# Pooled keys and values of two batches summed by TensorE, and a scale moved into the keys

## The chip, the cores and the metric

The kernel runs on one core of a Trainium2 chip. The metric is the device time in microseconds (us) of one execution.

## The reference

Attention over pooled keys and values, and then two feed-forward blocks. All inputs are fp32 or wider in DRAM (the weights come as 64-bit floats); q and k are drawn eight times larger than v.

```python
q, k, v: (8 batches, 8 heads, 576 rows, 64)
k_p = k.reshape(B, H, 72, 8, 64).mean(axis=3)      # v_p likewise
scores = (q @ k_p^T) / sqrt(64)
attn = softmax(scores, axis=-1)
x = (attn @ v_p) as (4608 tokens, 512)
h = ((x @ w1) * (x @ w2)) @ w3 @ w_out1            # 512 -> 1024 -> 512
y = relu(h @ w_in)**2 @ w_out                      # 512 -> 2048 -> 512
```

## The kernel before, in words

There are 4608 tokens in nine blocks of 512 (`TB`); a batch has 576 tokens, in five query tiles of 128 rows or 64 (`QT`), the first two and the last three of which form a half. Work goes in three parts that overlap.

*The fold.* `fold` multiplies w3 with the first w_out beforehand. `conv_w3` and `conv_wo` read 64-bit weights (`load64`, into `raw` tiles), ScalarE and four VectorE instructions of `to32` make two fp32 parts of each (tiles `v` for w3, summed into `wo`), and TensorE transposes the parts of w3 by fp32 matmuls with the identity (L542) and multiplies with wo (L565). The first group takes three blocks of w3 rows at once, the later ones one each. `load_split` converts the first half of w1 and w2 in the fold's later part.

*Attention.* `build_tasks` writes out a list of small steps; `tick`, which is called after every few matmuls, takes the next 0.6 to 0.7 of them, so that attention is spread among the matmuls of the other parts. For each batch `load_k` and `load_v` bring 128 pooled rows at a time, 8 x 64 numbers each (2 KB in a row), into tiles of a pool of three that the weights use as well, and VectorE sums each with one reduce (L248). GpSimd doubles the sums of k, `pe_kt` transposes them on TensorE, and copies put them in block-diagonal form into `kbd`. The sums of v are split by VectorE into a high and a low part (`vhl`), and 16 short DMAs per batch put them into `vl` (the first 128 pooled rows of each pair of heads) and `vr` (the 16 rows left). Then for each query tile `pe_s` makes scores of four heads at a time, their maximum (L351), its product with -scale (L352) and the exponentials (L354); `pe_t` transposes them and `pe_av` multiplies with `vl` and `vr`. For batches below `EARLY` = 2, q is loaded in natural layout and transposed on TensorE (L313); for the others VectorE transposes it.

*The token blocks.* `stage_ab` and `stage_w` run the first feed-forward block, from TensorE's view 24 matmuls of 512 columns for w1 and w2 and 12 for the folded weight, then `stage_h`, `stage_o` and `pair_group` the second. The second half of w1 and w2 (`fh1`) is converted while the first token block runs, stored to DRAM (L185) and read back in the order of use through a ring of eight tiles (`fetch`, `un`, L195). That ring stands empty until the fourth step of the first block.

Instructions are put in order per engine by a scheduler that follows the code's order unless a step would wait. Nearly all DMAs go through SP's queue, which issues in order; an instruction that waits for a buffer holds up those behind it.

Of the kernel before, what the change touches and what calls it, by code (L numbers as in the profile page):

```python
# [29 lines left out]
def attn_moe_moe2_kernel(  # L30
# [77 lines left out]
    def f32(ap):  # L108
        return ap.bitcast(F32)
# [98 lines left out]
    vl = at_p.tile([P, 2, NP, 2, D], F32R, tag="vl", name="vl")  # L208
    vr = at_p.tile([RR, NP, 2, D], F32R, tag="vr", name="vr")
    kbd = at_p.tile([P, NP, 2, SP], F32, tag="kbd", name="kbd")  # L210
    att = [at_p.tile([P, H * SP], F32, tag=f"att{i}", name=f"att{i}") for i in range(2)]

    def setup_consts():
        make_identity(nc, ident)
        nc.gpsimd.memset(f32(vl), 0.0)
        nc.gpsimd.memset(f32(vr), 0.0)
        nc.gpsimd.memset(kbd, 0.0)
        nc.gpsimd.memset(vp, 0.0)


    xt = {}
# [8 lines left out]
    atts = {}  # L230
    sums = {}
    rems = {}
    def kv_rows(j):
        return P if j < NJ - 1 else JL

    def load_kv(src, b, dst, j):
# [10 lines left out]
                    r[c * RM:(c + 1) * RM], flat[c * 2 * SP + P:(c + 1) * 2 * SP])  # L247
        nc.vector.reduce_sum(dst[:n], r[:n].rearrange("p r d -> p d r"), axis=AX.X)  # L248

    def load_k(b):  # L250

        for j in range(NJ):
            load_kv(k, b, kp[:, j, 0, :], j)
        nc.gpsimd.tensor_copy(kp[:, :NJ - 1, 1, :], kp[:, :NJ - 1, 0, :])
        nc.gpsimd.tensor_copy(kp[:JL, NJ - 1, 1, :], kp[:JL, NJ - 1, 0, :])

    def load_v(b):


        for j in range(NJ):  # L260
            load_kv(v, b, vp[:, j, :], j)
        nc.vector.tensor_copy(vhl[:, 0].bitcast(F32R), vp)
        nc.vector.tensor_sub(vp.bitcast(F32R), vp, vhl[:, 0])
        for par, (r0, r1) in enumerate(((0, SP), (SP, P))):
            for i in range(2):
                nc.sync.dma_start(f32(vl)[r0:r1, i, :, par, :], vhl[r0:r1, i, :NP, :])
        for c in range(NP):
            for i in range(3):
                r0 = i * RB + c % 2 * RM
                nc.sync.dma_start(  # L270
                    f32(vr)[r0:r0 + RM, c, 1, :], vhl[c * RM:(c + 1) * RM, i // 2, NP, :])
        done.add(("v", b))

    def pe_kt(b, part):


        ps = ps_at.tile([P, TB], F32, tag="at", name="ps_kt")
        n = (NJ - 1) * P
        c0 = (H - 1) * SP
        if part == 0:  # L280
            for j in range(NJ - 1):
                nc.tensor.transpose(
                    ps[:, j * P:(j + 1) * P], kp[:, j].rearrange("p a d -> p (a d)"), ident)
            nc.scalar.copy(kbd[:D, :, 0, :], runs(ps[:D], 0, 2 * SP, NP, SP))
            nc.scalar.copy(kbd[D:, :NP - 1, 1, :], runs(ps[D:], SP, 2 * SP, NP - 1, SP))
            nc.scalar.copy(kbd[D:, NP - 1, 1, :n - c0], ps[D:, c0:n])
            return
        nc.tensor.transpose(
            ps[:, :JL], kp[:JL, NJ - 1].rearrange("p a d -> p (a d)"), ident[:JL, :JL])
        nc.vector.tensor_copy(kbd[D:, NP - 1, 1, n - c0:], ps[D:, :JL])  # L290
        if b + 1 < B:
            load_k(b + 1)

    def runs(ap, off, step, n, w):

        a = ap[:, off:off + (n - 1) * step + w]
        return bass.AP(tensor=a.tensor, offset=a.offset, ap=[a.ap[0], [step, n], [1, w]])
# [29 lines left out]
    def pe_s(g, half):  # L327
# [17 lines left out]
        if half == 0:  # L345
            sums[g] = at_p.tile([P, H], F32, tag="sm", name="sm", bufs=2)
        sm = sums[g]

        scale = 1.0 / (POOL * D ** 0.5)

        nc.vector.reduce_max(mx[:n], sv, axis=AX.X)  # L351
        nc.vector.tensor_scalar(mx[:n], mx[:n], -scale, None, op0=ALU.mult)  # L352
        for h in range(NP):
            nc.scalar.activation(  # L354
                av[:, h0 + h], sv[:, h], ACTF.Exp, bias=mx[:n, h:h + 1], scale=scale,
                accum_out=sm[:n, h0 + h:h0 + h + 1])
        if half == 0:
            return
# [67 lines left out]
    def build_tasks():  # L426
# [24 lines left out]
        for g in range(NG):  # L451
# [9 lines left out]
                sc(g + 1)  # L461
            if i == HALF[hf][0]:
                put_pend(len(pend))
            for part in range(2):
                put(lambda g=g, part=part: pe_t(g, part))
                put_pend()
# [47 lines left out]
    def fold():  # L514
# [33 lines left out]
        for fs in groups:  # L548
# [3 lines left out]
            for h in range(nm // nh):  # L552
# [8 lines left out]
                for m in range(h * nh, (h + 1) * nh):  # L561
                    if first:
                        conv_wo(m)
                    for f in fs:
                        nc.tensor.matmul(  # L565
                            acc_w[f], w3t[f][:, m, :], wo_t[m // 2][:, m % 2, :],
                            start=m == 0, stop=m == nm - 1)
                        tick()
                    n += 1
                    if n == 4:  # L570
                        start_attention()
                    if n == 6:
# [17 lines left out]
    def stage_ab(i, u):  # L590
# [1 line left out]
        cs = slice(c * P, (c + 1) * P)  # L592
        pss = []
        if (i, u) == (0, TB // P - 1):
            until(lambda: not fh1)
            for _ in range(RING):
                fetch()
        for nm_ in ("w1", "w2"):
# [439 lines left out]
```

## Time and profile before

| | |
|---|---|
| median of three runs | 1645.61 us (1643.55 to 1647.1) |
| profiled execution, its own time | 1649.5 us |
| span of the profiled execution | 1647.6 us |
| TensorE busy (matmuls / weight loads) | 1583.2 us (96%) / 1261.8 us (77%) |
| VectorE busy | 940.3 us (57%) |
| ScalarE busy | 549.3 us (33%) |
| GpSimd busy | 164.8 us (10%) |
| mean granted TensorE clock | 0.987 of full speed |
| SP's DMA queue | 213888 packets, 212.28 MB |

The time is that of the whole execution, the span runs from its first to its last instruction. Shares are over the whole span; the stretches differ, so what an edit is worth is read from the stretch that it lies in. A granted clock of 1.0 is 2.4 GHz and 0.5 is 1.2 GHz.

### The profile page before, as it was taken

The numbers are of one execution on the slowest core, as the hardware profiler recorded it, in microseconds if no ns is written. First come the engines' busy times: TensorE is split into PE (matmuls) and PEld (weight loads), VectorE is DVE, ScalarE is ACT, GpSimd is POOL, SyncE is SP. The second block draws the span as 40 slices with busy tenths as digits, with TensorE's granted clock in tenths as the row PEclk, the third lists the DMA queues.
The fourth block names the chain that finished last, engine by engine and source line by source line (L and its number), as shares of the span: only waits on it lengthen the run. The fifth ranks groups of instructions, "written<-read, shape, count | busy, mean of one in ns | idle before, by whom it ended". The sixth has DMA issues, their size and how long they took to land.

```text
span 1647.6 us, 20821 instructions
## 1 busy us (share of the span) xinstructions
PE 1583.2 (96%) x7136; PEld 1261.8 (77%) x7136; DVE 940.3 (57%) x1658; ACT 549.3 (33%) x1485; POOL 164.8 (10%) x202
## 2 busy tenths in 40 slices
PE   7889789989999999999899999999999999999998
PEld 5456578777778778788688888888888888888887
DVE  8798756665765555636742535464546455645542
ACT  4454425444444343434322321132113211331121
POOL 1132301211111111112410000000000000000000
PEclk9999899999999999999999999999999999999999
DMA  8454575736475825542634444342444244414410
GB/s 261 142 156 131 158 212 139 205 105 188 126 201 156 261 72 163 142 123 65 222 102 118 134 131 126 117 129 82 128 119 128 83 127 123 123 43 130 127 64 26
DMA packets 218601, 222.00 MB, mean 135 GB/s; under 512 B 93056, under 2 KB 134016, under 8 KB 218496
## 3 DMA queue, kind: packets, MB, share of 16 engines
q1 hardware_dynamic: 213888, 212.28, 44.4%
q10 hardware_dynamic: 4608, 8.39, 1.4%
q8 instruction: 57, 0.93, 0.2%
q14 instruction: 48, 0.39, 0.1%
HBM read 179.31 MB, written 38.80 MB: 132 GB/s over the span
## 4 chain that ended last, share of the span: by engine, by line
PE 50%; DMA 0%; ACT 0%; issue 0%; DVE 0%; DVEq 0%
PE o L162 24%; PE ps_a L861 5%; PE ps_c L861 5%; PE ps_d L861 5%; PE ps_h L162 3%; PE ps_w L162 3%; PE ps_b L861 3%; PE acc L162 2%; DMA out_dram<-st 0%; DVE st L778 0%; ACT raw L136 0%; ACT st L780 0%; ACT asb L615 0%; DVEq L778 0%; ACT wt L113 0%
## 5 line engine op out<-in xcount | busy, mean ns | idle before, releaser
L162 PE MATMUL o<-wt,gt 128*128 128x512 f32 x1728 | 413.6, 394 | 0.0
L162 PEld LDWEIGHTS o<-wt,gt 128*128 128x128 f32 x1728 | 323.8, 188 | 77.1 <-ACT gt L113 1.2
L162 PE MATMUL ps_w<-x,un 128*128 128x512 f32 x864 | 222.2, 405 | 16.2 <-DMA un<-u_w 10.2
L162 PE MATMUL ps_w<-x,wt 128*128 128x512 f32 x864 | 228.6, 405 | 6.5 <-ACT x L415 2.3
L162 PE MATMUL acc<-gt,Wt 128*128 128x512 f32 x864 | 219.5, 397 | 1.0 <-ACT st L646 1.0
L162 PEld LDWEIGHTS ps_w<-x,un 128*128 128x128 f32 x864 | 163.2, 193 | 52.5 <-DMA un<-u_w 11.7
L162 PEld LDWEIGHTS ps_w<-x,wt 128*128 128x128 f32 x864 | 157.8, 190 | 42.0 <-DVE x L418 5.0
L162 PEld LDWEIGHTS acc<-gt,Wt 128*128 128x128 f32 x864 | 159.6, 189 | 35.1 <-ACT st L646 1.8
L354 ACT ACTIVATE att<-ps_s,mx 128x72 f32<-128x72 f32 (+1 forms) x320 | 98.2, 319 | 88.3 <-DVE mx L352 86.0
L861 PE MATMUL ps_a<-x2o,un 128*128 128x512 f32 x384 | 98.4, 391 | 0.0
L861 PE MATMUL ps_c<-x2o,un 128*128 128x512 f32 x384 | 97.5, 389 | 0.0
L861 PE MATMUL ps_d<-x2o,un 128*128 128x512 f32 x384 | 97.4, 389 | 0.0
L886 ACT ACTIVATE r<-ps_a 128x512 f32<-128x512 f32 x32 | 19.2, 599 | 232.6 <-PE ps_a L861 232.6
L619 DVE TENSOR_TENSOR gf<-asb,ps_w 128x512 f32<-128x512 f32 x72 | 49.3, 684 | 72.1 <-PE ps_w L162 68.3
L113 ACT CAST gt<-gf 128x512 fp32r<-128x512 f32 x88 | 54.9, 624 | 98.3 <-DVE gf L619 80.4
L114 DVE TENSOR_TENSOR gt<-gf,gt 128x512 fp32r<-128x512 f32 x88 | 68.6, 779 | 33.1 <-ACT gt L113 31.9
L114 DVE TENSOR_TENSOR gt<-gb,gt 128x512 fp32r<-128x512 f32 x64 | 43.8, 690 | 74.2 <-ACT gt L113 74.0
L861 PEld LDWEIGHTS ps_a<-x2o,un 128*128 128x128 f32 x384 | 72.1, 188 | 16.1
L861 PEld LDWEIGHTS ps_c<-x2o,un 128*128 128x128 f32 x384 | 72.1, 188 | 15.1
L861 PEld LDWEIGHTS ps_d<-x2o,un 128*128 128x128 f32 x384 | 72.1, 188 | 15.0
L362 POOL TENSOR_TENSOR att<-att,sm 128x576 f32<-128x576 f32 (+1 forms) x40 | 48.7, 1218 | 283.5 <-DVE sm L361 166.6
L113 ACT CAST gt<-g 128x512 fp32r<-128x512 f32 x64 | 39.9, 624 | 110.2 <-DVE g L732 86.1
(120 smaller groups left out, 1986.8 us busy)
## 6 DMA issues: line engine op xcount, KB each, us to landing
un<-u_w SPq DMA_DIRECT2D x144, 256.0 KB
un<-u_A SPq DMA_DIRECT2D x128, 256.0 KB
un<-u_S SPq DMA_DIRECT2D x128, 256.0 KB
raw<-in_moe_w_dram SPq DMA_DIRECT2D x32, 512.0 KB
raw<-in_moe_w_out_dram SPq DMA_DIRECT2D x24, 512.0 KB
out_dram<-st SPq DMA_DIRECT2D x36, 256.0 KB
kv<-in_k_dram SPq DMA_DIRECT2D x32, 256.0 KB
kv<-in_v_dram SPq DMA_DIRECT2D x32, 256.0 KB
```

The source lines that it names most:

```text
L113: nc.scalar.copy(hi, src)
L114: (eng or nc.vector).tensor_sub(lo, src, f32(hi))
L162: (lambda a=a, b=b, i=i: nc.tensor.matmul(ps, a, b, start=first and i == 0, stop=last and i == n - 1))
L354: nc.scalar.activation(av[:, h0 + h], sv[:, h], ACTF.Exp, bias=mx[:n, h:h + 1], scale=scale, accum_out=sm[:n, h0 + h:h0 + h + 1])
L362: nc.gpsimd.tensor_mul(av, av, sm[:n].unsqueeze(2).to_broadcast([n, H, SP]))
L619: nc.vector.tensor_mul(gf, asb, pss[1])
L861: nc.tensor.matmul(bank[bk], l, r, start=first and j == 0, stop=j == len(todo) - 1, skip_group_check=True)
L886: nc.scalar.activation(r, bank["a"], ACTF.Relu)
```

## The change

For the first two batches (`b < EARLY`) the pooled sums are made by TensorE. `load_early` loads row j of each group of eight, for all heads: eight tiles of 72 partitions x (8 heads x 64), taken from the ring of eight that the weights use later. `pe_kt` then multiplies the eight tiles of a pair of heads with the identity and accumulates in PSUM, which sums and transposes at once. `pe_v` sums v in the same way with `moved`, a shifted identity that puts the sums on the partitions that `vl` and `vr` want, and splits from PSUM. `moved` lies in the tile `vhl`, which later batches need for their own sums. The waiting place of the ring's first fetch now also asks that v of batch 1 is done. The two other edits hold for all batches: the scale is multiplied into `kbd`, and the maximum is negated by the reduce itself, so that L352 goes.

```diff
+    ones = vhl.rearrange("p i j d -> p (i j d)")[:SP]
+    moved = ones[:, :SP + P]
+    moved_r = ones[:, SP + P:SP + P + 2 * RR].rearrange("p (x r) -> p x r", x=2)
+    scale = 1.0 / (POOL * D ** 0.5)
...
-        nc.gpsimd.memset(vp, 0.0)
+        nc.gpsimd.memset(vhl, 0.0)
+        nc.gpsimd.tensor_copy(moved[:, SP:2 * SP], ident[:SP, :SP])
+        for x in range(2):
+            for i in range(3):
+                c0 = i * RB + x * RM
+                nc.gpsimd.tensor_copy(moved_r[:, x, c0:c0 + RM], ident[:SP, P - SP:SP])
...
+    def load_early(src, b):
+        early[src is k, b] = ts = []
+        s4 = src[b].rearrange("h (s r) d -> s h r d", r=POOL)
+        for j in range(POOL):
+            r = ring.tile([P, 2, 2, P], F32, tag="unit", name="kv_e")
+            t = r.rearrange("p a b c -> p (a b c)")[:SP]
+            nc.sync.dma_start(t.rearrange("p (h d) -> p h d", d=D), s4[:, :, j, :])
+            ts.append(t)
+
+    def pe_v(b, part):
+        ts = [t.rearrange("p (c a d) -> p c a d", a=2, d=D) for t in early[False, b]]
+        ps = ps_at.tile([P, TB], F32, tag="at", name="ps_v")
+        if part == 0:
+            pv = ps.rearrange("p (c a d) -> p c a d", a=2, d=D)
+            for a in range(2):
+                for j, t in enumerate(ts):
+                    nc.tensor.matmul(
+                        pv[:, :, a, :], moved[:, (1 - a) * SP:(1 - a) * SP + P], t[:, :, a, :],
+                        start=j == 0, stop=j == POOL - 1)
+            hi, lo = (vl[:, i].rearrange("p c a d -> p (c a d)") for i in range(2))
+            split(hi, lo, ps)
+            return
+        pr = ps[:RR, :NP * D].rearrange("p (c x d) -> p c x d", x=2, d=D)
+        for x in range(2):
+            for j, t in enumerate(ts):
+                nc.tensor.matmul(
+                    pr[:, :, x, :], moved_r[:, x], t[:, x::2, 1, :],
+                    start=j == 0, stop=j == POOL - 1)
+        pr = ps[:RR, :NP * D].rearrange("p (c d) -> p c d", d=D)
+        nc.scalar.copy(vr[:, :, 1, :], pr)
+        dl = vr[2 * RB:, :, 1, :]
+        nc.vector.tensor_sub(dl, pr[2 * RB:], f32(dl))
+        done.add(("v", b))
...
     def pe_kt(b, part):
+        if b < EARLY:
+            if part == 0:
+                kts[b] = ps_at.tile([P, TB], F32, tag="at", name="ps_kt")
+            ps = kts[b]
+            for hp in range(part * NP // 2, (part + 1) * NP // 2):
+                for j, t in enumerate(early[True, b]):
+                    nc.tensor.matmul(
+                        ps[:, hp * SP:(hp + 1) * SP], t[:, hp * P:(hp + 1) * P],
+                        ident[:SP, :SP], start=j == 0, stop=j == POOL - 1)
+            if part:
+                for a in range(2):
+                    nc.scalar.mul(
+                        kbd[a * D:(a + 1) * D, :, a, :],
+                        ps[a * D:(a + 1) * D, :NP * SP].rearrange("p (c s) -> p c s", s=SP), scale)
+                if b == 0:
+                    load_v(0)
+                load_k(b + 1)
+            return
...
-            nc.scalar.copy(kbd[:D, :, 0, :], runs(ps[:D], 0, 2 * SP, NP, SP))
+            nc.scalar.mul(kbd[:D, :, 0, :], runs(ps[:D], 0, 2 * SP, NP, SP), scale)
...
-        nc.vector.reduce_max(mx[:n], sv, axis=AX.X)
-        nc.vector.tensor_scalar(mx[:n], mx[:n], -scale, None, op0=ALU.mult)
+        nc.vector.reduce_max(mx[:n], sv, axis=AX.X, negate=True)
...
-                av[:, h0 + h], sv[:, h], ACTF.Exp, bias=mx[:n, h:h + 1], scale=scale,
+                av[:, h0 + h], sv[:, h], ACTF.Exp, bias=mx[:n, h:h + 1],
...
+            if b < EARLY and hf == 0 and i < 2:
+                put(lambda b=b, i=i: pe_v(b, i))
...
-                    if n == 6:
-                        load_v(0)
...
-            until(lambda: not fh1)
+            until(lambda: not fh1 and ("v", EARLY - 1) in done)
```

Two places show what the scheduler makes of it. On SP's queue, from the first load on, the kernel before has these rows (`raw` are weights, `kv` the pooled rows of k and v, `q_nat` is q):

```order
L125 DMA raw<-in_moe_w_dram 128x1024 x3
L125 DMA raw<-in_moe_w_out_dram 128x1024 x4
L241 DMA kv<-in_k_dram 128x512 x3
L310 DMA q_nat<-in_q_dram 128x8x64 x2
L125 DMA raw<-in_moe_w_dram 128x1024 x3
L125 DMA raw<-in_moe_w_out_dram 128x1024
L241 DMA kv<-in_k_dram 128x512
L241 DMA kv<-in_k_dram 64x512
```

and the changed kernel these (`kv_e` are the tiles of `load_early`):

```order
L125 DMA raw<-in_moe_w_dram 128x1024 x3
L125 DMA raw<-in_moe_w_out_dram 128x1024 x4
L274 DMA kv_e<-in_k_dram 72x8x64 x8
L387 DMA q_nat<-in_q_dram 128x8x64 x2
L125 DMA raw<-in_moe_w_dram 128x1024 x5
L125 DMA raw<-in_moe_w_out_dram 128x1024
L274 DMA kv_e<-in_v_dram 72x8x64 x8
L125 DMA raw<-in_moe_w_out_dram 128x1024 x2
L387 DMA q_nat<-in_q_dram 128x8x64 x2
L387 DMA q_nat<-in_q_dram 64x8x64
L125 DMA raw<-in_moe_w_out_dram 128x1024
L125 DMA raw<-in_moe_w_dram 128x1024 x3
```

All of k of batch 0 now stands ahead of q and the next weights, and all of v ahead of the last three wo blocks.

On TensorE's queue the last matmuls of the fold's first group stood like this before:

```order
L337 MATMUL ps_s<-kbd,qT 128x144 x4
L565 MATMUL ps_w<-wo,w3t 128x512 x3
L313 MATMUL ps_q<-ident,q_nat 128x128 x8
L313 MATMUL ps_q<-ident,q_nat 128x64 x4
L337 MATMUL ps_s<-kbd,qT 128x144 x4
L565 MATMUL ps_w<-wo,w3t 128x512 x3
L384 MATMUL ps_t<-ident,att_102 128x128 x4
```

and now like this (L640 is the multiplication with wo, L390 the transpose of q, L414 the scores, L617 the transpose of w3, L285 the first part of `pe_v`):

```order
L640 MATMUL ps_w<-wo,w3t 128x512 x3
L390 MATMUL ps_q<-ident,q_nat 128x128 x2
L640 MATMUL ps_w<-wo,w3t 128x512 x5
L390 MATMUL ps_q<-ident,q_nat 128x128 x6
L640 MATMUL ps_w<-wo,w3t 128x512
L390 MATMUL ps_q<-ident,q_nat 128x64 x4
L414 MATMUL ps_s<-kbd,qT 128x144 x2
L640 MATMUL ps_w<-wo,w3t 128x512 x2
L414 MATMUL ps_s<-kbd,qT 128x144 x2
L640 MATMUL ps_w<-wo,w3t 128x512
L617 MATMUL ps_w_592<-ident,v_584 128x128
L285 MATMUL ps_v<-kv_e,vhl 128x4x64 x16
```

The sums of k stand earlier on this queue, among the transposes of w3; the sums of v come when the first group has ended, and the transpose of the first query tile has moved behind them.

## Rows read from the trace of the kernel before

**Rows 1.** Stretches: start:end length, each engine's busy us, granted clock, DMA share, GB/s

```profile
10.00:64.40 54.40, 49.09 (x224) 33.06 (x225) 52.09 (x101) 23.60 (x67) 5.77 (x10) 0.94 0.76 223
64.40:137.00 72.60, 64.87 (x313) 39.93 (x311) 62.92 (x121) 39.39 (x124) 17.85 (x22) 1.00 0.48 142
137.00:213.20 76.20, 58.60 (x271) 45.00 (x269) 55.65 (x114) 36.08 (x132) 22.91 (x24) 0.89 0.54 150
213.20:580.00 366.80, 355.26 (x1666) 285.63 (x1667) 229.74 (x458) 151.75 (x509) 55.11 (x76) 0.99 0.62 175
580.00:1647.00 1067.00, 1054.64 (x4667) 857.68 (x4665) 536.83 (x862) 295.12 (x653) 60.27 (x62) 1.00 0.38 114
```

**Rows 2.** TensorE's waits, 64.4 to 137 and 137 to 213.2: total, times, longest

```profile
PE ps_w L542 <- DVE v L138: 4.8, 4, 2.0
...
PE ps_w L162 <- DMA un<-u_w: 6.5, 2, 4.8
```

**Rows 3.** Timeline of TensorE, and two stretches around 54 us

```profile
45.91 2.84 PE L565 MATMUL ps_w<-wo,w3t 128*128 128x512 f32 x6 [0.83 <-DVE wo L528]
55.08 5.24 PE L565 MATMUL ps_w<-wo,w3t 128*128 128x512 f32 x6 [0.59 <-DVE wo L528]
...
47.30:54.00 6.70, 4.52 (x23) 2.91 (x22) 6.63 (x13) 4.43 (x20) 1.83 (x4) 0.93 0.71 195
54.00:60.00 6.00, 5.41 (x9) 2.20 (x8) 5.61 (x13) 2.54 (x16) 0.41 (x2) 0.50 0.82 228
```

**Rows 4.** VectorE's groups up to 220 us, and its k reduces from 10 to 64.4

```profile
L248 DVE TENSOR_REDUCE kp<-kv 128x64 f32<-128x512 f32 x12 | 12.1, 1040 | 0.0
L352 DVE TENSOR_SCALAR mx<-mx 128x4 f32<-128x4 f32 x18 | 5.1, 286 | 0.1
L352 DVE TENSOR_SCALAR mx<-mx 64x4 f32<-64x4 f32 x4 | 1.7, 434 | 0.0
...
L248 DVE TENSOR_REDUCE kp<-kv x10: 1015/1040/1074, 23.0 to 47.2; 128x64 f32<-128x512 f32 x8, 64x64 f32<-64x512 f32 x2
```

**Rows 5.** Stretches 12 to 20 and 8 to 10 us, and the packets of the first

```profile
12.00:20.00 8.00, 8.00 (x44) 6.89 (x44) 8.00 (x18) 2.59 (x5) 0.00 (x0) 1.00 1.08 282
DMA packets 2772, 2.25 MB, mean 282 GB/s; under 512 B 2159, under 2 KB 2159, under 8 KB 2772
...
8.00:10.00 2.00, 0.00 (x0) 0.00 (x0) 1.90 (x5) 0.78 (x3) 0.00 (x0) 1.00 1.04 424
```

**Rows 6.** TensorE's small fp32 matmuls: ns min/median/max by line and tile, and timeline

```profile
L542 PE MATMUL ps_w<-ident,v x256: 272/275/581, 6.6 to 125.5; 128*128 128x128 f32 x128
L313 PE MATMUL ps_q<-ident,q_nat x40: 221/272/329, 28.3 to 121.7; 128*128 128x128 f32 x32, 64*128 64x64 f32 x8
...
19.66 8.83 PE L565 MATMUL ps_w<-wo,w3t 128*128 128x512 f32 x20
121.44 0.46 PE L313 MATMUL ps_q<-ident,q_nat 64*128 64x64 f32 x4
122.35 0.60 PE L282 MATMUL ps_kt<-ident,kp 128*128 128x128 f32 x4
124.04 1.73 PE L542 MATMUL ps_w<-ident,v 128*128 128x128 f32 x14
```

**Rows 7.** Timeline of TensorE on the weights read back

```profile
198.29 2.92 PE L162 MATMUL ps_w<-x,un 128*128 128x512 f32 x6 [4.80 <-DMA un<-u_w]
206.61 1.68 PE L162 MATMUL ps_w<-x,un 128*128 128x512 f32 x6
```

**Rows 8.** Stretches after 213 us, and who waits for the maximum's multiplication

```profile
340.00:350.00 10.00, 6.39 (x32) 4.95 (x31) 9.75 (x19) 4.37 (x15) 4.04 (x5) 1.00 0.40 105
350.00:360.00 10.00, 10.00 (x39) 8.31 (x40) 7.15 (x14) 3.06 (x11) 0.00 (x0) 0.83 0.18 36
410.00:420.00 10.00, 8.66 (x38) 5.93 (x37) 9.94 (x22) 4.14 (x16) 2.90 (x4) 1.00 0.84 265
...
ACT att L354: 86.0, 51
```

More of the change, by code (lines that the diff above doesn't have):

```diff
@@ L232, in attn_moe_moe2_kernel @@
     rems = {}
+    kts = {}
     def kv_rows(j):
@@ L248, in load_kv @@
         nc.vector.reduce_sum(dst[:n], r[:n].rearrange("p r d -> p d r"), axis=AX.X)
+    early = {}
+    def load_early(src, b):
[30 more added lines that the diff above has]
+        done.add(("v", b))
     def load_k(b):
+        if b < EARLY:
+            load_early(k, b)
+            return
         for j in range(NJ):
@@ L257, in load_v @@
     def load_v(b):
+        if b < EARLY:
+            load_early(v, b)
+            return
         for j in range(NJ):
@@ L274, in pe_kt @@
     def pe_kt(b, part):
+        if b < EARLY:
+            if part == 0:
[14 more added lines that the diff above has]
+                load_k(b + 1)
+            return
         ps = ps_at.tile([P, TB], F32, tag="at", name="ps_kt")
@@ L283, in pe_kt @@
                     ps[:, j * P:(j + 1) * P], kp[:, j].rearrange("p a d -> p (a d)"), ident)
-            nc.scalar.copy(kbd[:D, :, 0, :], runs(ps[:D], 0, 2 * SP, NP, SP))
-            nc.scalar.copy(kbd[D:, :NP - 1, 1, :], runs(ps[D:], SP, 2 * SP, NP - 1, SP))
-            nc.scalar.copy(kbd[D:, NP - 1, 1, :n - c0], ps[D:, c0:n])
+            nc.scalar.mul(kbd[:D, :, 0, :], runs(ps[:D], 0, 2 * SP, NP, SP), scale)
+            nc.scalar.mul(kbd[D:, :NP - 1, 1, :], runs(ps[D:], SP, 2 * SP, NP - 1, SP), scale)
+            nc.scalar.mul(kbd[D:, NP - 1, 1, :n - c0], ps[D:, c0:n], scale)
             return
@@ L289, in pe_kt @@
             ps[:, :JL], kp[:JL, NJ - 1].rearrange("p a d -> p (a d)"), ident[:JL, :JL])
-        nc.vector.tensor_copy(kbd[D:, NP - 1, 1, n - c0:], ps[D:, :JL])
+        nc.vector.tensor_scalar(kbd[D:, NP - 1, 1, n - c0:], ps[D:, :JL], scale, None, op0=ALU.mult)
         if b + 1 < B:
@@ L347, in pe_s @@
         sm = sums[g]
-        scale = 1.0 / (POOL * D ** 0.5)
-        nc.vector.reduce_max(mx[:n], sv, axis=AX.X)
-        nc.vector.tensor_scalar(mx[:n], mx[:n], -scale, None, op0=ALU.mult)
+        nc.vector.reduce_max(mx[:n], sv, axis=AX.X, negate=True)
         for h in range(NP):
             nc.scalar.activation(
-                av[:, h0 + h], sv[:, h], ACTF.Exp, bias=mx[:n, h:h + 1], scale=scale,
+                av[:, h0 + h], sv[:, h], ACTF.Exp, bias=mx[:n, h:h + 1],
                 accum_out=sm[:n, h0 + h:h0 + h + 1])
```

## The prediction

> **What bounds the kernel now.** I read the windows first, cut at four events: the first matmul group of the fold ends at 64.4 us, the fold at 137, the weights of the second half of w1 and w2 stop running short at 213.2, and the attention work thins out at 580. In [rows 1] the reader is to see where TensorE is not full. From 10 to 64.4 it stands idle 54.4 - 49.1 = 5.3 us, up to 137 72.6 - 64.9 = 7.7, up to 213.2 76.2 - 58.6 = 17.6, up to 580 366.8 - 355.3 = 11.5; then 12.4 us in 1067. So the last two thirds are TensorE's own and the change can win only ahead of 580. VectorE is the other full engine at the front: 52.1 of 54.4 us, then 62.9 of 72.6, then 55.7 of 76.2 [rows 1].
>
> Next the waits: in the fold TensorE waits most for the weights that VectorE converts (v, L138 and L141), and between 137 and 213.2 for `un`, the weights that come back from DRAM, 6.5 us in two waits [rows 2]. VectorE converts those too, so both waits end with it. Last the timeline: at 55 us TensorE has waited for a wo block (L528) that VectorE brings late, and the six matmuls behind this wait take 5.24 us where six took 2.84 at 45.9 [rows 3]. The window 54 to 60 has a granted clock of 0.50, the lower of TensorE's two levels (1.2 GHz), after 6.7 us in which TensorE was busy 4.5 [rows 3].
>
> **What the change removes.** VectorE loses 20 reduces of 1.04 us (two batches, five each for k and v) and the small multiplication of the maximum, by 220 us 5.1 for eighteen and 1.7 for four of the short tiles [rows 4]; what else goes and comes on it nearly cancels. That is 27 us of the 171 that it is busy from 10 to 213.2. SP's queue loses the 16 short copies into vl and vr of each early batch, for which I count nothing. ScalarE and GpSimd change by a few us and are busy less than half of these stretches [rows 1]; GpSimd's seven copies that build the moving matrix come right after its memsets, long ahead of the first v matmul, and would cost only if k or v came first. The scale rides on copies that are there already.
>
> **What it adds on TensorE.** Each fp32 matmul is two records in the trace: the code makes 128 of L542, the trace shows 256 [rows 6]. Twenty records of 512 columns take 8.83 us and six 2.84, so one each (8.83 - 2.84) / 14 = 0.428 us [rows 3, 6]; fourteen of 128 columns give, without the last one's own 0.275, (1.73 - 0.275) / 13 = 0.112 [rows 6].
> - v of a batch: 16 matmuls of 256 columns, 32 x 0.214 = 6.9 us, and 16 of 128 columns, 32 x 0.112 = 3.6 us: 10.5 us.
> - k of a batch: 32 matmuls of 72 columns, 64 records. No row has that size. At the slope of the others a record streams for 0.061 us (3.9 us in all); if its weights set the pace as with 128 columns it is 0.112 (7.2 us). The nearest row, four transposes of 64 columns in 0.46 us, gives (0.46 - 0.221) / 3 = 0.08 [rows 6]; I take 5.1 us. The five transposes that go take 0.7 (four in 0.60 [rows 6]), so 4.4 net.
>
> Both batches: 2 x 14.9 = 29.8 us (27.4 to 34). This is the price, and it can only come back because TensorE stands idle 30.6 us between 10 and 213.2.
>
> **What it moves: the loads.** k and v of the early batches now come in packets of 256 bytes (one head's row), eight loads for a batch, where a row of 2 KB came before. The q loads have such packets. In the window 12 to 20 us 2159 packets under 512 B and 613 larger ones moved 2.25 MB with the DMA engines full [rows 5]: the large ones are 1.70 MB, 4.0 us at the 424 GB/s of the window 8 to 10; the small 0.55 MB took the other 4 us, 138 GB/s. So a k load of 1.18 MB takes 8.5 us instead of 2.8. SP's rows put all eight of k ahead of q and the next w3 loads, where three loads of 256 KB stood (1.9 us): q and w3 land up to 6.6 us later. The eight loads of v then wait for TensorE's last reading of k, and three wo blocks and three q loads queue behind them; the block that TensorE waits for at 55 us now [rows 3] should land by then all the same.
>
> The Trainium skill (DMA: Bandwidth & Descriptors, section Why a DMA increments its semaphore by 16 and not by 1) says that a DMA gets the largest number of engines up to 16 that divides the outermost dimension of both sides; 72 rows would get 12. By it the load takes 11.4 us as an estimate, and the first stretch would end some 3 us later than below. No row here shows it.
>
> **The sum, by stretch.**
> - 10 to 64.4: TensorE's 49.1 us, less 2.4 of lost clock, plus 4.4 for k, is 51.1. VectorE loses ten reduces of k by 47.2 [rows 4] and five of v, which delay the last wo blocks; against it stand the 6.6 us by which w3 lands later, covered in part by the k matmuls and by the matmuls on wo that run up to 28.5 [rows 6]. I leave 1.3 of the 5.3 idle: 52.4, **-2.0** (from -3.3, no idle time, to +6.6, the late loads uncovered).
> - 64.4 to 137: 64.9 + 10.5 + 4.4 = 79.8; of the 7.7 idle I leave 3, since VectorE is no longer full: 82.8, **+10.2** (+8 to +15).
> - 137 to 213.2: two groups of six matmuls take 2.92 us where six take 1.68 at the full clock [rows 7], so 58.6 - 2.5 + 10.5 = 66.6. The conversions of w1 and w2 end earlier while TensorE gets there later, so the wait for `un` and the low clock around it should go; with 1.6 idle 68.2, **-8.0** (-9.5 to 0, if v's loads, again ahead of weights in SP's queue, renew the wait).
> - After 213.2: most multiplications of the maximum lie here, and ScalarE waited 86 us for all 80 [rows 8]; TensorE seldom waits for ScalarE. The clear places are 340 to 350 and 410 to 420, where VectorE is busy 9.75 and 9.94 of 10 us and TensorE loses 3.6 and 1.3 us, and 1.7 to the clock (0.83) after the first [rows 8]. I take half of it, **-3.2** (-6 to +2).
>
> Sum -3.0. Against the profiled execution's 1649.5 that is 1646.5; it lies 3.9 above the median of the runs, 1645.61, so the forecast is **1642.6 us**, on the border of what a measurement of this kernel can tell from no change, 0.2% or 3.3 us.
>
> **The rivals.**
> - *The matmuls find no cover* (slower, 30%): the idle time is made of short waits on data, and new matmuls in TensorE's in-order queue come on top. For it: from 64.4 to 137 TensorE is busy nine tenths already [rows 1]. Against it: the waits named end with VectorE. My sum gives back 4.0 + 4.7 + 16.0 of idle time and 4.9 of clock; if two fifths of these 29.6 us fail, the time is 1642.6 + 11.8 = 1654. It decides from 6.3 us. The small packets alone, 6.6 us in the first stretch in place of -2.0, give 1651; they show as ScalarE waiting for the DMA of w3 or wo and TensorE behind it, before 65 us.
> - *Every gap fills* (10%): the 1.3, 3 and 1.6 us left above and the other half of the gaps after 213.2 go too, 1633.5.
> - *It does nothing measurable* (10%): the 30 us added and those given back cancel, 1645.6.
>
> The granted clock stood at 0.50 from 54 to 60 us after a stretch of a third idle [rows 3]. A rule of the Trainium skill (TensorE: Matmul & The Clock Gate, section What's actually happening) has the low level as the default that activity releases; the trace agrees, and by it each gap that stays would cost again behind its end.
>
> **How the numbers follow.** My forecast has half of the chance; its own spread of 1635 to 1650 (k's cost, the first and the last stretch) falls 30 to 19 to 1 on faster, no change and slower. The matmuls without cover have 30 (28 slower, 2 no change), every gap filled 10, nothing measurable 10 (1, 7, 2). So faster 0.41, no change 0.28, slower 0.31. The range from 1633 to 1657 leaves out a tenth on either side.
>
> **What would show it.** Right: the fold ends 6 to 10 us later than 137, with TensorE idle under 5 us in its second stretch; the wait for `un` is under 2 us; VectorE is busy about 144 us from 10 us to the point that was 213.2; k records of 0.06 to 0.11 us. Wrong: TensorE waiting for early k or v, or for wo, over 5 us before 70; a low clock in a new place; the wait for `un` still there. If v's records of 256 columns cost more than 0.214 us, the price itself is wrong, by 0.13 us for each 2 ns.

## The result: slower, and the profile after

The changed kernel takes 1667.96 us (median of four, 1662.74 to 1673.81) where the kernel before takes 1646.36 (1643.55 to 1647.24) beside it: 1.0137 of its time, interval 1.0117 to 1.0156. The forecast was 1642.6, and 1657 the upper end of its range. The profiled execution of the changed kernel is the slowest of the four, 1673.81 at a mean granted clock of 0.985 (another took 1671.14 at 0.985, the other two 1664.78 at 0.991 and 1662.74 at 0.990), so the sizes below are some 6 us above the typical ones, and a part of the low clock seen in it is missing in two of the four.

The page, first its engines:

```profile
span 1672.0 us, 21158 instructions
PE 1620.5 (97%) x7382; PEld 1300.8 (78%) x7382; DVE 909.5 (54%) x1556; ACT 549.7 (33%) x1487; POOL 163.4 (10%) x205
```

The windows of the changed kernel, cut at the same events as [rows 1]: the first group's end, the fold's end, the same work done as at 213.2 before, and 600 for 580 (columns as there):

```profile
10.00:71.40 61.40, 56.13 (x275) 42.25 (x276) 40.26 (x80) 21.08 (x54) 2.49 (x3) 0.89 0.68 187
71.40:167.90 96.50, 89.44 (x434) 63.79 (x433) 70.04 (x126) 45.61 (x139) 25.73 (x27) 0.89 0.48 139
167.90:232.70 64.80, 60.24 (x306) 49.06 (x304) 44.94 (x88) 29.15 (x93) 16.23 (x18) 1.00 0.56 167
232.70:600.00 367.30, 355.09 (x1696) 284.23 (x1696) 218.54 (x421) 155.19 (x543) 55.26 (x78) 1.00 0.59 168
600.00:1672.00 1072.00, 1058.88 (x4675) 860.97 (x4673) 532.77 (x841) 295.43 (x655) 59.54 (x63) 0.99 0.38 113
```

The first stretch is 7.0 us longer than before, the second 23.9, the third 11.4 shorter, the other two together 4.9 longer (1439.3 us to the end, 1434.4 before), some 3 us of it attention work that the cut leaves to them. So the loss lies in the fold, most of it in the second stretch, where the granted clock is 0.89 instead of 1.00 (0.89 instead of 0.94 in the first). Windows of 2 us show where:

```profile
30.00:32.00 2.00, 2.00 (x20) 2.00 (x20) 1.52 (x3) 1.51 (x3) 0.00 (x0) 1.00 0.38 150
32.00:34.00 2.00, 2.00 (x12) 2.00 (x12) 1.83 (x5) 0.00 (x0) 0.00 (x0) 0.53 0.01 4
...
138.00:140.00 2.00, 0.58 (x2) 0.00 (x0) 0.98 (x1) 0.34 (x1) 0.00 (x0) 1.00 0.37 135
...
144.00:146.00 2.00, 2.00 (x12) 2.00 (x11) 1.27 (x3) 1.50 (x3) 1.07 (x1) 0.50 0.79 246
160.00:162.00 2.00, 2.00 (x6) 1.43 (x6) 0.26 (x1) 0.62 (x1) 0.00 (x0) 0.54 0.93 209
162.00:164.00 2.00, 2.00 (x9) 1.19 (x8) 1.83 (x4) 1.68 (x9) 0.00 (x1) 1.00 0.58 139
```

At 32 us the clock falls to half although TensorE is busy 2.00 of 2.00 us. Near 141 it falls behind a wait of 2 us, before the first record of k of batch 1, and stays low through these records until 162. TensorE's timeline says what runs then:

```profile
29.38 7.20 PE L342 MATMUL ps_kt<-ident,kv_e 72*128 72x72 f32 x44 [0.24 <-ACT qT L393]
...
36.89 3.10 PE L342 MATMUL ps_kt<-ident,kv_e 72*128 72x72 f32 x14
...
141.60 2.07 PE L640 MATMUL ps_w<-wo,w3t 128*128 128x512 f32 x2
143.47 6.94 PE L342 MATMUL ps_kt<-ident,kv_e 72*128 72x72 f32 x32
150.20 2.01 PE L640 MATMUL ps_w<-wo,w3t 128*128 128x512 f32 x2
152.00 6.94 PE L342 MATMUL ps_kt<-ident,kv_e 72*128 72x72 f32 x32
```

and for v, in two other lines of it:

```profile
71.80 7.14 PE L285 MATMUL ps_v<-kv_e,vhl 72*128 72x256 f32 x32
...
96.31 3.66 PE L294 MATMUL ps_v<-kv_e,vhl 72*96 72x128 f32 x32
```

The 72-column records of k take 0.10 to 0.11 us at first (20 in the 2 us from 30 to 32) and 0.217 at half the clock (6.94 / 32), and the fold's own matmuls between them pay too: a pair of 512 columns takes 2.0 us instead of 1.0. v's records cost what was forecast, 7.14 + 3.66 us against 6.9 + 3.6. Last TensorE's waits of the changed kernel, from 10 to 72 and from 150 to 260:

```profile
PE ps_w L617 <- DVE v L141: 3.6, 3, 2.4
PE ps_w L640 <- DVE wo L603: 3.6, 1, 3.6
...
PE ps_t L462 <- DVE vr L300: 1.4, 1, 1.4
```

The wait for `un` of [rows 2] is gone, as forecast; the longest wait for a wo block is 3.6 us, where it was 0.83 before [rows 3].

### The profile page after: what moved, and what is told of

Read it like the earlier page. It is cut to its first block, busy times and chain, and to the rows that moved or that the text cites. A ratio compares the mean times of both kernels' runs of the same rounds, so it can differ in the third digit from the quotient of the medians.

```text
span 1672.0 us, 21158 instructions
## 1 busy us (share of the span) xinstructions
PE 1620.5 (97%) x7382; PEld 1300.8 (78%) x7382; DVE 909.5 (54%) x1556; ACT 549.7 (33%) x1487; POOL 163.4 (10%) x205
## 4 chain that ended last, share of the span: by engine, by line
PE 71%; DVE 6%; DMA 4%; SPq 2%; ACT 2%; issue 2%; POOL 1%; ACTq 0%; DVEq 0%; POOLq 0%
PE o L162 24%; PE ps_w L162 15%; PE acc L162 8%; PE ps_a L934 5%; PE ps_c L934 5%; PE ps_d L934 5%; PE ps_h L162 3%; PE ps_b L934 3%; DMA rq<-in_moe_w_in_dram 2%; PE ps_s L414 1%; PE ps_av L162 1%; DVE w L138 1%; DMA x2d<-st 1%; DVE vhl L262 1%; PE ps_t L457 1%
## 5 line engine op out<-in xcount | busy, mean ns | idle before, releaser
L162 PEld LDWEIGHTS ps_w<-x,wt 128*128 128x128 f32 x864 | 156.3, 189 | 34.8 <-DVE x L491 4.1
```

The lines of the kernel that those rows point to most:

```text
L162: (lambda a=a, b=b, i=i: nc.tensor.matmul(ps, a, b, start=first and i == 0, stop=last and i == n - 1))
```

## The experiments

Theory A was that k's small matmuls lose the clock, and that this is the loss. Rival B was that TensorE's added work finds no cover, whatever its clock. Rival C was the small packets and the new order of loads. Expectations stand as they were written before each run.

To compare fronts, I cut each profiled execution at the first store of the first token block's result (the first DMA to `x2d`). The table has the length from 10 us to that point, TensorE's busy time in it, and as idle the rest of the length. Ratios are to the kernel before as measured beside each run (medians of 1645.5 to 1646.9 us):

| kernel | median us | ratio (95%) | length | busy | idle |
|---|---|---|---|---|---|
| before | 1646.4 | 1 | 271.6 | 239.7 | 31.9 |
| changed | 1668.0 | 1.0137 | 294.3 | 274.9 | 19.4 |
| e1 scale only | 1645.6 | 1.0001 (0.9992–1.0010) | 269.0 | 234.8 | 34.2 |
| e2 v only | 1659.5 | 1.0086 (1.0072–1.0100) | 281.0 | 251.2 | 29.8 |
| e3 k only | 1665.7 | 1.0120 (1.0106–1.0135) | 291.8 | 258.4 | 33.4 |
| e4 k wide | 1656.5 | 1.0063 (1.0050–1.0075) | 280.9 | 263.7 | 17.2 |
| e5 k in eight steps | 1670.5 | 1.0143 (1.0130–1.0157) | 286.3 | 268.5 | 17.8 |
| e6 k wide, v late | 1649.6 | 1.0021 (1.0012–1.0029) | 274.0 | 259.9 | 14.1 |
| e7 k wide only | 1671.5 | 1.0157 (1.0144–1.0171) | 296.8 | 251.7 | 45.1 |
| e8 two of eight | 1641.2 | 0.9971 (0.9962–0.9980) | 257.6 | 234.6 | 23.0 |
| e9 k with 128 columns | 1661.5 | 1.0088 (1.0073–1.0103) | 274.7 | 257.6 | 17.1 |
| e10 sums on GpSimd | 1664.8 | 1.0109 (1.0096–1.0122) | 284.9 | 249.0 | 35.9 |
| e11 v late | 1672.1 | 1.0156 (1.0143–1.0170) | 291.5 | 272.6 | 18.9 |
| e12 pairs on VectorE | 1655.6 | 1.0055 (1.0043–1.0067) | 271.7 | 250.4 | 21.3 |
| e13 the same, v alone | 1663.8 | 1.0102 (1.0085–1.0119) | 281.4 | 256.4 | 25.0 |
| e14 v wide | 1655.5 | 1.0051 (1.0036–1.0065) | 282.2 | 264.0 | 18.2 |
| e15 e6, two of eight | 1647.8 | 1.0015 (1.0006–1.0023) | 266.3 | 241.3 | 25.0 |
| e16 tree on VectorE | 1652.6 | 1.0034 (1.0022–1.0045) | 270.5 | 235.7 | 34.8 |
| e17 e4, pairs on VectorE | 1649.1 | 1.0012 (1.0003–1.0021) | 275.1 | 251.8 | 23.3 |
| e18 e4, two of eight | 1643.9 | 0.9986 (0.9974–0.9997) | 262.6 | 241.5 | 21.1 |

The rest of the span, from the store to the end, lies between 1360 and 1376 us in all of them (1366.0 before, 1367.7 changed), and does not follow the front: where the order of steps shifts, gaps of a few us open and close up to some 850 us. A difference under about 8 us in one profile is not put down to one cause here.

**The parts by themselves (e1, e2, e3).** e1 keeps the sums on VectorE and takes only the scale and the negated maximum:

```diff
-        nc.vector.reduce_max(mx[:n], sv, axis=AX.X)
-        nc.vector.tensor_scalar(mx[:n], mx[:n], -scale, None, op0=ALU.mult)
+        nc.vector.reduce_max(mx[:n], sv, axis=AX.X, negate=True)
```

> Only the scale in the pooled keys and the negated maximum; the sums of k and v stay on VectorE as before. All theories agree: VectorE loses one small multiplication per four heads, and my sum for the part after 213 us gave -3.2. Expected 1643 us (1640 to 1647), against 1646.4 before. If it is slower than before, the two small edits carry part of the loss, and the other theories are priced too high.

Measured 1645.6, no change: VectorE has 15 us less to do (925.7 on the page, 940.3 before) and the time does not see it.

e2 takes `if b < EARLY` out of `load_k` and `pe_kt`; e3 takes it out of `load_v` and drops `pe_v`. In both, `load_v(0)` stands at `n == 6` again.

> v of the first two batches on TensorE, k back on VectorE with its whole rows of 2 KB, the two small edits kept. Theory A (the loss is the clock that falls to half while TensorE runs k's 72-column matmuls, and k's records that cost 0.11 us instead of 0.08): no low clock between 140 and 162 us, and 1645 us (1640 to 1650), as my sum had it without k. Rival B (TensorE's added work finds no cover, whatever its clock): v is 21 of the 29.8 us added, so about 17 of the loss stays: 1660. Rival C (256-byte packets and the order of loads and of ScalarE's work): v keeps half of the small packets, loss about 10: 1653.

> k of the first two batches on TensorE as in the change, v back on VectorE and its copies; the two small edits kept. Theory A: the granted clock is 0.5 for about 10 us around k of batch 0 and again around k of batch 1, and most of the loss is here: 1659 us (1655 to 1665). Rival B: k is 9 of the 29.8 us added: 1651. Rival C: half of the small packets, and all of those ahead of q and w3: 1655, with TensorE waiting for data before 70 us, and no difference by the clock.

Measured 1659.5, rival B's number, and 1665.7, just above A's range. Theory A has its low clock in e3 around k of batch 0 but not in k of batch 1, and v alone costs 14 us more than e1, as rival B said and A did not: up to the first store TensorE is busy 251.2 - 234.8 = 16.4 us longer than in e1, and its idle time gives back 4.4. So A is not the whole loss.

**The clock of k (e4, e9, e5).** e4 sums k with the identity as weights and 512 columns of k moving, and transposes the sums afterwards:

```diff
+                for j, t in enumerate(early[True, b]):
+                    nc.tensor.matmul(
+                        ps[:SP], ident[:SP, :SP], t, start=j == 0, stop=j == POOL - 1)
...
+                nc.scalar.copy(kts[b], ps[:SP])
...
+            for hp in range(NP):
+                nc.tensor.transpose(
+                    ps[:, hp * SP:(hp + 1) * SP], kts[b][:, hp * P:(hp + 1) * P], ident[:SP, :SP])
```

> The change, but k summed by eight matmuls of 512 moving columns with the identity as weights (16 records of 0.43 = 6.9 us a batch, the same TensorE time at the full clock as 64 records of 0.11), then a copy and four transposes of 72 columns. Loads, ring, order of DMAs and TensorE's busy time are the change's own. Theory A: the clock stays at 1.0 through k of both batches, and the fold's end comes 10 to 14 us earlier: 1655 us (1651 to 1659). Rivals B and C: nothing that they blame is changed, so 1668 as the change (1665 to 1671), whatever the clock does.

e9 changes a single width, with PSUM columns to match:

```diff
-                        ps[:, hp * SP:(hp + 1) * SP], t[:, hp * P:(hp + 1) * P],
-                        ident[:SP, :SP], start=j == 0, stop=j == POOL - 1)
+                        ps[:, hp * P:(hp + 1) * P], t[:, hp * P:(hp + 1) * P],
+                        ident[:SP], start=j == 0, stop=j == POOL - 1)
```

> The change with one number different: k's matmuls multiply with 128 columns of the identity's first 72 rows instead of 72 columns (the other 56 add zeros in PSUM). The same 64 records a batch, the same weights, the same order and loads; by the trace of v's transposes a record of 128 columns takes 0.112 us at the full clock, as the 72-column ones did before their clock fell (0.11). Theory A (few columns per weight load lose the clock): clock 1.0 through k of batch 0, k of batch 0 in 7 us instead of 11, and 1657 us (1654 to 1661), so more columns make it faster. If the clock falls with any run of small fp32 matmuls that change their weights, nothing moves: 1668 (1665 to 1671).

Measured 1656.5, A's number, and 1661.5, half a us above A's range, against 1668.0. In e4 the clock is 1.00 through both batches; TensorE's timeline on batch 1 there (sixteen records in 7.09 us, 0.44 each, and a pair of the fold in 1.0 again):

```profile
138.31 7.09 PE L340 MATMUL ps_kw<-kv_e,ident 72*72 72x512 f32 x16
...
147.21 1.07 PE L643 MATMUL ps_w<-wo,w3t 128*128 128x512 f32 x2
```

The windows of e9 at the place where the changed kernel's clock fell, and its records:

```profile
30.00:32.00 2.00, 2.00 (x20) 2.00 (x20) 1.55 (x3) 1.40 (x3) 0.00 (x0) 1.00 1.03 420
32.00:34.00 2.00, 2.00 (x20) 2.00 (x20) 1.92 (x4) 0.00 (x0) 0.00 (x0) 1.00 1.10 350
34.00:36.00 2.00, 2.00 (x20) 2.00 (x20) 1.86 (x4) 0.85 (x2) 0.00 (x0) 1.00 0.76 158
```

```profile
29.27 3.17 PE L342 MATMUL ps_kt<-ident,kv_e 72*128 72x128 f32 x26 [0.24 <-ACT qT L393]
```

Up to 32 us both kernels run the same rows, 26 records with the same weights behind the same matmuls; with 72 columns moving the clock falls there, with 128 it holds, and the wider record costs hardly more, (3.17 - 0.275) / 25 = 0.116 us without the last one's own 0.275. TensorE is busy 2.00 of 2.00 us in both; that doesn't tell the two apart. Behind 32 us e9 has the fold's transposes among k's records, so what follows there is not k's alone. e9's six runs lie between 1658.1 and 1666.6 and its profile is the fastest; they overlap the changed kernel's four (1662.7 to 1673.8), so that the clock holds is shown by the rows, and its 6.5 us of the median less surely.

The fall in batch 0 repeats: in e3, e5 and e11, which have the same 44 records there, the clock falls between 32 and 34 us too, with TensorE busy 2.00 of 2.00 us, and in e4, e6 and e7, with the wide form, it doesn't. Batch 1 is another matter. In e3 it has the same 64 records with a pair of the fold between, as the changed kernel has, and they run at the full clock, 0.115 us each; the clock falls only as the last of them end, near 153 (TensorE's timeline of e3, then its windows):

```profile
144.90 3.69 PE L334 MATMUL ps_kt<-ident,kv_e 72*128 72x72 f32 x32
148.42 1.07 PE L628 MATMUL ps_w<-wo,w3t 128*128 128x512 f32 x2
149.33 3.69 PE L334 MATMUL ps_kt<-ident,kv_e 72*128 72x72 f32 x32
```

```profile
150.00:152.00 2.00, 2.00 (x21) 2.00 (x19) 1.97 (x4) 0.00 (x0) 0.00 (x0) 1.00 0.43 126
152.00:154.00 2.00, 2.00 (x12) 1.17 (x11) 1.59 (x2) 0.81 (x2) 1.29 (x1) 0.80 0.38 136
```

In the changed kernel the clock was low before these records came, behind the wait of 2 us, and they did not bring it back. So A's mechanism is shown for batch 0; for batch 1 it is shown that the records can run at either clock.

e5 was to spread batch 1's k over eight steps:

> The change, with k's 32 matmuls of a batch handed out as eight steps of four instead of two of sixteen; only batch 1 comes out differently on TensorE (between the fold's matmuls instead of 32 records at a stretch). If it takes k's small matmuls standing together to lose the clock (theory A as it now stands), the low clock from 140 to 162 us goes and about 8 of the loss with it: 1660 us (1656 to 1664). If k's shape loses it wherever it stands: 1668 (1665 to 1671). Batch 0 keeps its low clock in both.

Measured 1670.5, and the run doesn't test what it was made for: the steps came after the fold and stood together there, as TensorE's timeline of e5 shows.

```profile
147.81 13.05 PE L343 MATMUL ps_kt<-ident,kv_e 72*128 72x72 f32 x64
```

The clock was 1.00 at their start and 0.50 from 148.8 to 172. In e11 the 64 stood together as well (139.4 to 150.1), and the clock fell among them, at 143. Whether small matmuls in fours between large ones keep the clock stays open; the nearest case is e3's two groups of 32 above.

**The order of loads (e6, e11, e7).** e6 is e4 with v of batch 0 and k of batch 1 loaded from `pe_v`, behind the last wo blocks on SP's queue:

```diff
     def pe_v(b, part):
+        if b == 0 and part == 0:
+            load_v(0)
+            load_k(1)
...
```

> The version with k in 512-column matmuls, with the loads of v of batch 0 and k of batch 1 issued behind the last wo blocks instead of ahead of three of them. There TensorE waited 5.5 us for wo before 59 us and ran some 4 us at the half clock behind it. Theory D (SP's queue: v's loads hold up wo): the wait is under 2 us, the first group ends at 65 to 66 us, and the time is 1649 us (1646 to 1652). Rival E (wo is late because ScalarE's conversion stands behind exponentials that wait for k): wo lands earlier but the wait stays, 1656 (1654 to 1658).

Measured 1649.6, theory D's number. In e4 v's eight loads stood on SP's queue for 14 us, wo blocks behind them. Issuing one took 0.30 us; for the rest SP waited for tiles of the ring, which come free as TensorE reads k. Then ScalarE's conversion of wo stood behind 16 small instructions of the exponentials. The first rows are of SP's queue in e4, then its issues by tile (ns, shortest, median and longest) and its waits from 25 to 60 us, then TensorE's waits up to 72 us in e4 and in e6:

```profile
30.94 14.13 SPq L274 DMA_DIRECT2D kv_e<-in_v_dram  x8
45.16 0.89 SPq L125 DMA_DIRECT2D raw<-in_moe_w_out_dram  x2
```

```profile
L274 SPq DMA_DIRECT2D kv_e<-in_v_dram x8: 300/301/326, 30.9 to 44.8; - x8
```

```profile
SPq L274 <- PE ps_kw L340: 18.1, 7, 7.5
```

```profile
PE ps_w L643 <- DVE wo L606: 5.5, 1, 5.5
```

```profile
PE ps_w L645 <- DVE wo L608: 0.2, 1, 0.2
```

e11 makes the same move in the change itself.

> The change with only the loads moved: v of batch 0 and k of batch 1 are issued behind the last wo blocks. With k in wide matmuls the same edit gave 7 us. If the late wo and the low clock of k are separate losses that add: 1661 us (1658 to 1664), the wait for wo at 59.8 us gone and the two low clocks still there. If the low clock before hides behind the wait for wo, as both delay the same matmuls: 1666 (1664 to 1669).

Measured 1672.1 where 1661 or 1666 was expected. The wait for wo fell to 0.2 us and the fold ended at 159.8 instead of 168.5, but up to the first store 6 us of it were lost again and behind it 8 more, in waits spread over both parts, none over 3 us up to 240, and in the low clock. e11's profile is the slowest of its five runs (1671.5 to 1679.3). A local gain was shown; that it reaches the end was not.

e7 is e3 with k in the wide form.

> k of the first two batches on TensorE in 512-column matmuls, v on VectorE as before. It fills the fourth field of a table: neither 1645.5, v alone 1659.5, both 1656.5. If the two parts add, 1642.5 (1640 to 1645), a gain. If k is covered only because v has left VectorE, its 7.5 us of TensorE a batch come on top: 1656 (1652 to 1660).

Measured 1671.5, far above both. With v on VectorE again, TensorE's two largest waits there are

```profile
PE ps_w L631 <- DVE wo L594: 8.7, 1, 8.7
```

```profile
PE ps_q L383 <- DMA q_nat<-in_q_dram: 10.5, 1, 10.5
```

19 us, for a wo block that stands behind k's loads of batch 1 on SP's queue and for q loads that stand behind the 16 copies into `vl` and `vr`, and the low clock behind each. e3 has the same two (5.2 and 10.4 us), so its 20 us are not the clock's alone.

**The price (e8, e18, e15).** The change, e4 and e6, each with only two of the eight tiles multiplied:

```diff
-                for j, t in enumerate(ts):
+                for j, t in ((0, ts[0]), (POOL - 1, ts[-1])):
```

> The change with only the first and the last of the eight tiles multiplied (the sums leave out six of eight rows); loads, VectorE's relief, copies and splits are the change's own. It takes three quarters of the added matmuls away, by the traces 16 us of v and 10 to 17 us of k with its low clock. If TensorE's price comes on top and VectorE's relief is worth little (rival B for v): 1668 - 16 - 14 = 1638 (1634 to 1643), and the relief together with the late loads is then worth about nothing, since 8 us of matmuls are left. If the loss is in loads and order (rival C): over 1655. If the relief were worth the 20 us that my sum took from the stretches up to 213 us: under 1632.

> The wide version with v's loads where the change has them, with only the first and the last of the eight tiles multiplied (the sums leave out six of eight rows). If the late loads took the gain back: 1641 (1637 to 1644), as the change with two of eight. If k's wide form did (its copy and its extra step on ScalarE): 1648 (1645 to 1651).

> The wide version with late v loads with only the first and the last of the eight tiles multiplied (the sums leave out six of eight rows): 26 us of TensorE's price less, nothing else changed. If the price is what ate the saving: 1628 us (1624 to 1634), that is, nearly all of the 26 us. If VectorE and the order set the pace again once TensorE has room, as with the change itself with two of eight (1641): 1638 (1634 to 1643).

Measured 1641.2 and 1643.9, rival B's number and the first of e18's two, and 1647.8, above both of e15's: taking three quarters of the price away brings 27 us in the change (with its low clock), 12.6 in e4 and 1.8 in e6. Up to the store TensorE is busy 40.3, 22.2 and 18.6 us less, and the front is 36.7, 18.3 and 7.7 us shorter. But e8 and e18 take away more than the price: k is read sooner, the ring's tiles come free sooner, v's loads have left SP's queue at 36.8 instead of 45.8 (34.9 instead of 45.1 in e18), and the wait for wo falls from 3.6 to 0.7 us (5.5 to 1.0). In e6 that wait was gone already. So the price and the order of loads act together, and these runs don't separate them. The three end within 7 us of each other, at best 5 under the kernel before, with a quarter of the price, some 8 us, still in.

**The sums elsewhere (e10, e12, e13, e14, e16, e17).** e10 is e6 with GpSimd adding eight tiles to two:

```diff
+        for n in (POOL // 2, POOL // 4):
+            for j in range(n):
+                nc.gpsimd.tensor_add(ts[j], ts[j], ts[j + n])
+        del ts[2:]
```

> The wide version with late v loads (1649.6), with GpSimd adding the eight tiles to two first (six adds of 72x512 a batch for k and for v, by the trace 1.3 us each; GpSimd is busy a tenth of the time), so that TensorE multiplies two tiles instead of eight. It takes 10 us of k and 16 us of v from TensorE. If TensorE's price is what is left of the loss: 1638 us (1633 to 1643), below the kernel before; VectorE then sets the pace again. Rival: GpSimd's adds come late or hold up what stands behind them on GpSimd (the sum of w1 and w2's parts, the normalized exponentials), or slow VectorE beside them: 1646 or more.

Measured 1664.8: the rival. The 24 adds take GpSimd 37.9 us, 1.59 each (the median is 1.27, the longest 6.10), and VectorE's instructions beside one are stretched, in e10 from 50 us on; behind 55.9 the same two take 0.69 again. Which of the rival's ways carries the loss, this run doesn't tell.

```profile
50.90 4.77 POOL L278 TENSOR_TENSOR kv_e<-kv_e 72x512 f32<-72x512 f32 x3
```

```profile
51.13 1.74 DVE L612 TENSOR_TENSOR wo<-wo,raw 128x512 f32<-128x512 f32 x1
52.80 1.75 DVE L141 SCALAR_TENSOR_TENSOR raw<-raw 128x512 f32<-128x512 uint32 x1
...
57.65 0.69 DVE L141 SCALAR_TENSOR_TENSOR raw<-raw 128x512 f32<-128x512 uint32 x1
58.38 0.69 DVE L612 TENSOR_TENSOR wo<-wo,raw 128x512 f32<-128x512 f32 x1
```

e12 adds pairs on VectorE in e6 (four adds, `nc.vector.tensor_add`, and TensorE multiplies four tiles), e13 does so for v alone; e14 sums v in eight 512-column matmuls and places the sums by four more. (In e14 the sums of v of batch 1 go over pooled keys of batch 2 in a shared tile, which changes that batch's output and none of the work.)

> The wide version with late v loads, with VectorE adding the eight tiles to four first (four adds of 72x512 for k and for v of a batch; by the trace an add of this size takes 0.69 us), so TensorE multiplies four. TensorE loses 3.5 us for k and 5.2 for v of a batch, 17 us in all, and VectorE gets 11 of the 27 us back. If TensorE's price is what is left of the loss: 1641 us (1636 to 1645), faster than the kernel before. If shifts of the order decide: no lower than 1648.

> The same for v alone: TensorE loses 10.4 us, VectorE gets 5.5. If price: 1644 us (1640 to 1647). If shifts of the order decide: no lower than 1648.

> The wide version with late v loads, with v summed once in eight matmuls of 512 columns, copied, and then placed by four matmuls with the shifted identity: 6.9 + 1.3 us a batch in place of 10.5, 4.6 us less on TensorE, VectorE's work unchanged, two copies more on ScalarE. If price: 1646.5 us (1644 to 1649). If shifts of the order decide, or the copy between the two steps holds TensorE up: 1650 or more.

Measured 1655.6, 1663.8 and 1655.5: all slower than e6, though TensorE is asked for 17, 10 and 5 us less. e16 is the change with e10's tree on VectorE, e17 is e4 with pairs on VectorE.

> The change with VectorE adding the eight tiles to two (six adds of 72x512 for k and for v of a batch, 0.69 us each by the trace, 16.6 us in all, of the 27 that the change took off it), and TensorE multiplying two tiles. TensorE's work is that of the change with two of eight tiles, 1641.2. If VectorE has room for the adds: 1642 to 1646, no slower than the kernel before. If the adds stand ahead of the weights' conversions on VectorE and TensorE waits for these again: 1650 or more.

> The wide version with v's loads where the change has them (1656.5), with VectorE adding pairs (four adds for k and for v of a batch) and TensorE multiplying four tiles, 17 us less. If the price counts in full in this order of loads: 1642 (1638 to 1646). If adds on VectorE cost as they did with the late loads (6 us more, not less): 1656 or more.

Measured 1652.6, in the range of the adds that stand ahead of the conversions, and 1649.1, between e17's two numbers. Each has one large wait up to 72 us, e16 for a wo block and e17 for q:

```profile
PE ps_w L644 <- DVE wo L607: 10.4, 1, 10.4
```

```profile
PE ps_q L397 <- DMA q_nat<-in_q_dram: 9.8, 1, 9.8
```

No version that makes the whole sums is faster than the kernel before. Of rival C, the order of loads is worth 7 us with k in the wide form (e4 to e6); no run takes away the small packets alone, so what they cost stays open.

## Why the prediction was wrong, point by point

- **The price of k** (5.1 us a batch, bounds 3.9 to 7.2) was the first step to fail. I took 0.08 us a record from a row of 64-column transposes. At the full clock it is 0.11, the upper bound. The bounds themselves left out that such records can run at half the clock: batch 0 took 7.20 + 3.10 + 0.56 + 0.34 = 11.2 us, batch 1 13.9, together 14.9 more than the 10.2 of the sum, and the fold's pairs between them another 3. In batch 0 the records themselves lost the clock (e9's rows); in batch 1 a wait ahead of them did. With k in the wide form (e4) 11.5 us of the median came back. "A low clock in a new place" stood under what would make the prediction wrong.
- **The idle time given back** (24.7 us in the first three stretches, and 4.9 of clock) was the second, and the larger. e4 has it alone: up to the first store its TensorE is busy 263.7 - 239.7 = 24.0 us more than before, where the sum had 24.9, but idle only 31.9 - 17.2 = 14.7 less, and with k at the full clock it still ends 14 us above the forecast. In the changed kernel, up to the first store TensorE's busy time rose by 274.9 - 239.7 = 35.1 us, where the sum had 29.8 - 4.9; the idle time fell by 12.5. 35.1 - 12.5 is the 22.7 us by which the store comes later, and the part behind it is 1.7 longer. VectorE did lose 31 us over the whole (909.5 on the page), though from 10 us to the end of the third stretch it is busy 155.2 where about 144 was the sign; the wait for `un` did go, with the third stretch at 64.8 us where 68.2 was forecast. But VectorE's relief became VectorE's idle time in the fold, which ended 31 us later, where 6 to 10 was the sign. It stood still 7.3 and 7.5 us at 23 and 35 us, in the changed kernel's timeline:

```profile
30.41 0.43 DVE L137 TENSOR_SCALAR v<-raw 128x512 uint32<-128x512 uint32 x1 [7.34 <-ACT raw L136]
...
42.66 0.43 DVE L137 TENSOR_SCALAR v<-raw 128x512 uint32<-128x512 uint32 x1 [7.51 <-PE ps_w L617]
```

  The first wait is for a conversion of w3 that ScalarE has queued behind the copy of q (L393, which had itself waited 8.5 us for TensorE's transposes of q), the second for transposes of w3 that stand behind k's matmuls on TensorE. Behind them a wo block came 3.6 us late at 59.8, and the clock from 59 to 64 was 0.66; that this wait comes from the order of loads e11 shows, where it is 0.2.
- **The loads.** The k load was forecast at 8.5 us, and the q and w3 loads up to 6.6 us late, hidden behind matmuls. From 14 to 18 us, with packets under 512 B alone, the queue moved 163 GB/s, so a k load takes 7.2 us; this part was about right. The 11.4 us by the Trainium skill's rule (DMA: Bandwidth & Descriptors, Why a DMA increments its semaphore by 16 and not by 1) did not come. How many engines a load got can't be read here, since the DMA share goes above 1, but loads of 72 rows (v, 40 to 42 us) and of 128 rows (q, 19.5 to 21) moved the same, 212 and 209 GB/s:

```profile
14.00:18.00 4.00, 4.00 (x22) 3.04 (x22) 4.00 (x9) 1.30 (x3) 0.00 (x0) 1.00 1.01 163
19.50:21.00 1.50, 1.50 (x5) 0.61 (x5) 1.50 (x4) 0.59 (x1) 0.00 (x0) 1.00 1.27 209
40.00:42.00 2.00, 2.00 (x10) 2.00 (x10) 0.00 (x0) 0.00 (x0) 0.00 (x0) 0.50 0.95 212
```

  That v's loads wait for TensorE's last reading of k, with wo blocks behind them, was foreseen; that the block of 55 us "should land by then all the same" was wrong, and cost 7 us, shown by e4 against e6, with k wide. With k as in the change (e11) the end did not move by it.
- **After 213 us** -3.2 was forecast for the shorter maximum; e1 measured nothing (1645.6 us, with 1645.5 beside it).
- **The rival "no cover"** (30%, 1654) was the right side, with another mechanism on top: with v alone (e2) 16.4 us of busy time made the front 12.0 longer than e1's and the time 14. Taking three quarters of the price out of e6 gained little, however (e15): its front is 7.7 us shorter and the part behind the store 8.3 longer, 3.6 of it busy time, at a mean granted clock of 0.992 where e6 had 0.997, and 4.7 idle time. Why e6 has no gain, and which waits a better order would remove, was not settled.

## What to carry to other kernels

Price a matmul by its shape's own row, and ask of a long run of small ones what the clock does beside them: busy time alone will not show it, and here padding to 128 columns or swapping the operands cost little and kept it. An engine's idle time is not a budget: of 30 us of short waits 12 came back here, since in-order queues (SP's loads, ScalarE's copies) hand the relieved engine new waits. Before moving work off a full engine, take most of the moved work out altogether and time that: here that left a gain of 5 us with a quarter of the work still in.

## What the runs showed of the hardware

- TensorE busy 2.00 of 2.00 us with 72-column fp32 records, whose weights change each time, fell from 2.4 to 1.2 GHz at 32 us with 0.24 us of idle time ahead of it; in the same place with 128 columns and 0.116 us a record it did not. In e3 the same records, in two groups of 32, ran at 2.4 GHz to the end. The Trainium skill (TensorE: Matmul & The Clock Gate, What's actually happening) has activity release the low level; the falls behind waits agree (0.50 behind the wait of 2 us near 141), and the fall at 32 us came without a wait of that kind.
- A VectorE instruction of 512 columns takes 0.69 us alone and up to 1.75 beside a GpSimd add of 512 columns (e10), so GpSimd's idle time was not free either.
- SP issued a 72x512 load in packets of 256 B in 0.30 us (e4); that eight of them held its queue for 14.13 us came from the waits for their tiles. A merged row of a queue has such waits in it.
- Loads in packets of 256 B moved 163 to 212 GB/s in the changed kernel, where the weights in large packets moved 424 before [rows 5].
